# Where the inverse row sums lie for the product that normalises P

## The chip, the core and the metric

The kernel runs on one core of one Trainium2 chip. The metric is device time in microseconds (us), the median of three runs; lower is better. A core has five engines with queues of their own: TensorE (PE in the profile, with its weight loads as PEld), VectorE (DVE), ScalarE (ACT), GpSimd (POOL) and SyncE (SP), which here issues the DMAs. They run side by side and wait for each other through semaphores. Two on-chip memories matter: SBUF, which all of them use, and PSUM, the banks into which matmuls write.

## What is computed

Causal windowed attention with a linear bias per head, and then a soft mixture of experts over all tokens:

```python
scores = scale * q @ k.T                                   # B=8, H=8, S=576, D=64
scores = where((rel >= 0) & (rel < 128), scores + bias, -1e9)
attn = exp(scores - scores.max(-1));  attn /= attn.sum(-1) + 1e-09
x = (attn @ v)            # reshaped to N=4608 tokens x 512
logits = x @ phi          # 32 slots
d = softmax(logits, over tokens);  slot_input = d.T @ x
slot_out[e] = relu(slot_input[e] @ w1[e]) @ w2[e]          # 8 experts x 4 slots
out = softmax(logits, over slots) @ slot_out
```

The change sits in `attn /= attn.sum(...)`.

## The kernel before

A tile is 128 queries of one batch entry (the fifth tile of an entry has 64). A tile's heads are worked in groups of four score matrices, so there are 72 groups; each group is a score tile of 128 x 4 x 128 values that count. The program first runs a loop over the 72 groups, and then a tail with the experts and the output.

The instructions of each engine stand in the order in which the code below calls them; nothing reorders them. In iteration `i` of the loop, with `new` = group i and `old` = group i-1:

- `softmax_front(new, old)`, nearly all on DVE: `merge` (L286) puts the masked halves of the scores together in PSUM, `total` (L309, on POOL) adds 1e-9 to the row sums of `old`, `rowmax` (L300) takes the maximum of each row and writes it, negated, into spare columns of the same PSUM tile, `inverse` (L313) makes reciprocals of the row sums of `old`, `bias` (L304) scales the maxima of `new` into `nb` in SBUF, and `normalise` (L317) multiplies P of `old`, 128 x 512 values in SBUF, by the inverse sums of their rows.
- `flip` and `split` of group i-3: PE transposes P into PSUM (L374), ACT copies it to SBUF (L380), POOL cuts it along the diagonal with two selections (L386, L388).
- `values` of group i-4: the matmuls with V (L410). After the second group of a tile DVE copies the result out (L424).
- `scores` of group i+1: PE (L261, L270).
- `expo(new)`: four exponentials on ACT (L359), each with a sum along its row; each shows as an ACTIVATE and an ACTIVATION_READ_ACCUMULATOR.
- on some iterations, further steps: transposes of finished tiles (L438, copied out at L447), and, when four tiles are finished (a pass), their logits (L456) and a running softmax over tokens (L464 to L522).

The score tile of group i is one of two PSUM tiles, taken in turn; each is two banks:

```python
173 |     s4s = [ps_s.tile([P, 4, 2 * P], F32, name=f"s4_{i}") for i in range(2)]
299 |         st[key]["mx"] = ranges(key, us)[:, :, 4 * P - 2:4 * P]
```

The scores take at most the first 448 of the 512 columns of a bank; the row maxima take the last two. `st[key]["rs"]` is a tile of four columns in SBUF, one of two buffers. Groups 0 and 1 are normalised by other branches (`first`, `eager`), and the last group is normalised behind the loop.

When the program is built, each instruction is given the semaphore waits that its operands need. For a PSUM bank these follow the bank, whatever columns of it are used.

Of the kernel before, what the change touches and what calls it, by code (L numbers as in the profile page):

```python
# [24 lines left out]
P = 128  # L25
# [47 lines left out]
def tile_attn_softmoe(  # L73
# [13 lines left out]
    nc = tc.nc  # L87
# [56 lines left out]
    st = {}  # L144
# [131 lines left out]
    ALL, LO, HI = slice(0, 4), slice(0, 2), slice(2, 4)  # L276
    EVEN, ODD = slice(0, 4, 2), slice(1, 4, 2)

    def merge(key, us=ALL):
        x = ranges(key, us).rearrange("p a (x y) -> p a x y", y=KB)  # L280
        m = x.shape[1]
        if key[1] < 4:
            to, of, keep = x[:, :, 0:6:5], x[:, :, 2:4], bc(mask.bitcast(I32), 1, m)
        else:
            to, of, keep = x[:, :, 0:8:4], x[:, :, 2:8:4], bc(bc(mask[:, 0].bitcast(I32), 1, 2), 1, m)
        nc.vector.copy_predicated(to, keep, of)  # L286
# [9 lines left out]
    def rowmax(key, us):  # L296
        if "nb" not in st[key]:
            st[key]["nb"] = work.tile([P, 4], F32, tag="nb", name="nb")
        st[key]["mx"] = ranges(key, us)[:, :, 4 * P - 2:4 * P]
        nc.vector.tensor_reduce(st[key]["mx"], merged(key, us), axis=AX.X, op=ALU.max, negate=True)  # L300

    def bias(key, us):
        nb = st[key]["nb"][:, us].rearrange("p (a u) -> p a u", u=2)
        nc.vector.tensor_scalar_mul(nb, st[key]["mx"], SCALE)  # L304

    def total(key, us, eng=None):
        if "rs" not in st[key]:
            st[key]["rs"] = work.tile([P, 4], F32, tag="rs", name="rs")
        (eng or nc.vector).tensor_scalar(  # L309
            st[key]["rs"][:, us], st[key]["sm"][:, us], EPS, 1.0, op0=ALU.add, op1=ALU.mult)  # L310

    def inverse(key, us):
        nc.vector.reciprocal(st[key]["rs"][:, us], st[key]["rs"][:, us])  # L313

    def normalise(key, us):
        p4, rs = st[key]["p4"][:, us], st[key]["rs"][:, us]
        nc.vector.tensor_tensor(p4, p4, bc(rs, 2, P), op=ALU.mult)  # L317

    def normalise_first(key, us):
        p4 = st[key]["p4"]  # L320
        for u in range(4)[us]:
            nc.scalar.mul(p4[:, u], p4[:, u], st[key]["rs"][:, u:u + 1])  # L322
# [3 lines left out]
    def filler():  # L326
        if fillers:
            fillers.pop(0)()

    def softmax_front(new, old):  # L330
        first, eager = number[old] == 0, 0 < number[old] < EAGER
        merge(new)
        filler()
        if not eager:
            total(old, ALL, nc.gpsimd)
        if first:
            inverse(old, ALL)
            normalise_first(old, LO)
        rowmax(new, ALL)
        filler()  # L340
        if not first and not eager:
            inverse(old, ALL)
        filler()
        bias(new, ALL)
        if eager:
            total(old, ALL)
            inverse(old, ALL)
        filler()
        normalise(old, HI if first else ALL)
# [262 lines left out]
    sums = area[:, 3]  # L612
# [161 lines left out]
    with tc.manual_schedule(engines=ORDERED):  # L774
        scores(0)
        loads(0)
        for i in range(n):
            new = groups[i]
            run("pre", i)
            if i:  # L780
                softmax_front(new, groups[i - 1])
            else:
                for us in (LO, HI):
                    merge(new, us)
                    rowmax(new, us)
                    bias(new, us)
                    expo(new, us)
            near = int(i < SKIP)
            if i + near >= FLAG and i != SKIP:
                flip(groups[i + near - FLAG])  # L790
                split(groups[i + near - FLAG])
            run("act", i)
            if i + near >= LAG and i != SKIP:
                values(groups[i + near - LAG])
                after_values(i, groups[i + near - LAG])
            if i + 1 < n:
                scores(i + 1)
            if i + 1 < n - 1:
                loads(i + 1)
            if i:  # L800
                expo(new)
            run("pe", i)
            load_weights_at(i)
            run("dve", i)
# [324 lines left out]
```

## Time and profile before

| | |
|---|---|
| median of 3 runs | 286.24 us (286.18 to 286.52) |
| the profiled execution | 286.09 us, of which the span from first to last instruction is 284.3 us |
| granted TensorE clock | 0.992 |
| loop over the groups | up to about 213 us of the span; the tail from there |
| busy share of the span | PE 91%, DVE 77%, ACT 67%, POOL 39% |

The busy shares are means over the loop and the tail. Rows of a timeline read: start in us, duration in us, engine, line, operation, out<-in, and in brackets how long the engine sat idle before and what ended that. An instruction may start some 0.1 us before the one ahead of it on its engine ends, where it need not wait for it.

### The profile page before, as it was taken

How to read it: one execution, taken by the hardware profiler on the slowest of the kernel's cores; microseconds unless marked ns; L12 is line 12 of the kernel's file. 1: busy time of each engine (PE TensorE's matmuls, PEld its weight loads, DVE VectorE, ACT ScalarE, POOL GpSimd, SP SyncE). 2: the span in 40 equal slices, each digit the busy share in tenths (PEclk: the TensorE clock that was granted, in tenths of full speed). 3: DMA queues.
4: the chain of work that ended last, by engine and by line, in shares of the span. 5: the costliest groups of instructions: out<-in, count | busy, mean ns of one | idle time of the engine just before them, and what ended most of it. 6: DMA issues, size and time to landing. Idle time of an engine off the chain costs nothing.

```text
span 284.3 us, 11675 instructions
## 1 busy us (share of the span) xinstructions
PE 257.5 (91%) x4575; PEld 180.7 (64%) x4575; DVE 218.6 (77%) x546; ACT 190.5 (67%) x780; POOL 111.7 (39%) x221
## 2 busy tenths in 40 slices
PE   7789898989899999998989998998989899999990
PEld 3567676767577677676667766766666443587750
DVE  1789998997998898899999899897973352656352
ACT  2868868887798887897897888887774411044460
POOL 3035734481574385265527526556452011000000
PEclk9999999999999999999999999999999999999996
DMA  5735368889786998889698778876565588999997
GB/s 167 238 110 153 115 173 250 255 247 295 252 277 184 303 303 262 257 265 285 221 298 283 255 236 280 268 212 218 166 213 199 172 257 296 417 416 373 376 357 295
DMA packets 36767, 72.49 MB, mean 255 GB/s; under 512 B 4413, under 2 KB 15337, under 8 KB 36713
## 3 DMA queue, kind: packets, MB, share of 16 engines
q1 hardware_dynamic: 35992, 71.25, 75.7%
q8 instruction: 36, 0.59, 0.8%
q10 hardware_dynamic: 720, 0.51, 0.6%
q14 instruction: 19, 0.15, 0.2%
HBM read 62.30 MB, written 9.44 MB: 252 GB/s over the span
## 4 chain that ended last, share of the span: by engine, by line
PE 44%; DVE 38%; ACT 9%; issue 3%; DMA 3%; POOL 1%; DVEq 0%; ACTq 0%; SPq 0%; POOLq 0%
DVE area L317 12%; DVE s L300 9%; PE xp L410 8%; ACT area L359 6%; PE op L967 5%; PE s L270 5%; DVE area L424 5%; PE hp L930 5%; DVE s L286 4%; PE po L992 4%; PE s L261 2%; PE lp L456 2%; PE pq L374 2%; DVE acc L522 2%; DMA area<-v_n 2%
## 5 line engine op out<-in xcount | busy, mean ns | idle before, releaser
L359 ACT ACTIVATE area<-s,nb 128x128 f32<-128x128 f32 x286 | 101.9, 379 | 21.6 <-DVE nb L304 20.2
L410 PE MATMUL xp<-area 128*64 128x128 f32 (+1 forms) x1104 | 71.7, 270 | 9.5 <-DVE area L424 6.6
L410 PEld LDWEIGHTS xp<-area 128*64 128x64 f32 x1104 | 54.5, 137 | 16.4 <-POOL area L388 5.0
L359 ACT ACTIVATION_READ_ACCUMULATOR area<-s,nb 128x1 f32 x286 | 62.2, 218 | 0.0
L317 DVE TENSOR_TENSOR area<-area,rs 128x512 f32<-128x512 f32 (+1 forms) x73 | 59.9, 821 | 1.7 <-ACT area L447 0.4
L270 PE MATMUL s<-kq 64*64 64x192 f32 (+2 forms) x1144 | 57.0, 316 | 0.0
L386 POOL TENSOR_SCALAR_AFFINE_SELECT area<-area 128x512 f32<-128x512 f32 (+1 forms) x57 | 42.7, 748 | 26.9 <-ACT area L380 26.3
L380 ACT COPY area<-pq 128x512 f32<-128x512 f32 (+1 forms) x72 | 42.5, 592 | 16.0 <-PE pq L374 14.3
L300 DVE TENSOR_REDUCE s<-s 128x4 f32<-128x512 f32 (+1 forms) x72 | 50.0, 694 | 2.2
L388 POOL TENSOR_SCALAR_AFFINE_SELECT area<-area 128x512 f32<-128x512 f32 (+1 forms) x57 | 46.5, 817 | 3.9
L270 PEld LDWEIGHTS s<-kq 64*64 64x64 f32 x1144 | 41.2, 139 | 3.4
L309 POOL TENSOR_SCALAR rs<-sm 128x4 f32<-128x4 f32 x70 | 13.5, 193 | 71.2 <-ACT area L359 69.8
L286 DVE COPY_PREDICATED s<-cst,s 128x256 f32<-128x256 int32 (+1 forms) x72 | 30.2, 419 | 4.8 <-PE s L270 4.4
L374 PE MATMUL pq<-unit_r,area 64*128 64x64 f32 x552 | 31.4, 234 | 1.9 <-ACT area L322 1.2
L374 PEld LDWEIGHTS pq<-unit_r,area 64*128 64x128 f32 x552 | 23.0, 140 | 11.6 <-issue 5.0
L261 PE MATMUL s<-ramp,pair_of 64*64 64x384 bf16 x286 | 27.0, 358 | 2.5 <-ACT area L359 2.0
L424 DVE COPY area<-xp 128x512 f32<-128x512 f32 (+1 forms) x38 | 24.1, 633 | 3.6 <-PE xp L410 3.4
L447 ACT COPY area<-pq 128x512 f32<-128x512 f32 x34 | 20.2, 594 | 0.3 <-PE pq L432 0.3
L261 PEld LDWEIGHTS <-pair_of 64*64 64x64 bf16 x288 | 9.5, 106 | 15.7 <-issue 12.0
L438 PEld LDWEIGHTS pq<-unit_r,area 64*128 64x128 f32 x264 | 10.7, 138 | 13.2 <-issue 11.7
L994 ACT COPY ob<-po 128x512 f32<-128x512 f32 x19 | 10.4, 592 | 11.4 <-PE po L992 11.4
L994 DVE COPY ob<-po 128x512 f32<-128x512 f32 x17 | 11.2, 686 | 6.6 <-PE po L992 4.4
(164 smaller groups left out, 276.6 us busy)
## 6 DMA issues: line engine op xcount, KB each, us to landing
w<-w SPq DMA_DIRECT2D x53, 512.0 KB, 5.4
out<-ob SPq DMA_DIRECT2D x36, 256.0 KB, 3.6
kq<-q_t SPq DMA_DIRECT2D x69, 128.0 KB, 3.3
kq<-k_t SPq DMA_DIRECT2D x32, 256.0 KB, 3.4
area<-v_n SPq DMA_DIRECT2D x31, 256.0 KB, 4.5
area<-w SPq DMA_DIRECT2D x8, 512.0 KB, 4.9
area<-v_n SPq DMA_DIRECT2D x12, 128.0 KB, 5.2
kq<-w SPq DMA_DIRECT2D x3, 512.0 KB, 5.6
```

The source lines that it names most:

```text
L261: nc.tensor.matmul(dst[strip], lhsT=pair_of[rows, int(t == 0), strip], rhs=src, start=True, stop=False)
L270: nc.tensor.matmul(parts[par][KB * jj:KB * jj + KB, second * u + KB * skip:second * u + WIN], lhsT=qt[rows, jj if t < 4 else j, KB * h:KB ...
L286: nc.vector.copy_predicated(to, keep, of)
L300: nc.vector.tensor_reduce(st[key]["mx"], merged(key, us), axis=AX.X, op=ALU.max, negate=True)
L317: nc.vector.tensor_tensor(p4, p4, bc(rs, 2, P), op=ALU.mult)
L359: nc.scalar.activation(s["p4"][:, u], src, AF.Exp, bias=s["nb"][:, u:u + 1], scale=SCALE, accum_out=s["sm"][:, u:u + 1],)
L374: nc.tensor.transpose(s["pt"][:, 2 * (u % 2) + u // 2, r], s["p4"][rows, u], ident[rows, rows])
L380: nc.scalar.copy(pa[:, us].rearrange("p u (r w) -> p u r w", r=2), s["pt"][:, us])
L386: nc.gpsimd.affine_select(prev, own, [[-step, m], [0, 4], [-1, KB]], ALU.is_gt, 0.0, base=-i0, channel_multiplier=1)
L388: nc.gpsimd.affine_select(own, own, [[step, m], [0, 4], [1, KB]], ALU.is_ge, 0.0, base=i0, channel_multiplier=-1)
L410: nc.tensor.matmul(xp[D * par:D * par + D, j, 0:w], lhsT=v_slot[b, t - 1 + ph][:, D * h:D * h + D], rhs=src[:, :, par, i] if t < 4 else sr ...
L424: nc.vector.tensor_copy(dst, src[:, :, 0:w])
```

## The change

For the groups that the loop normalises in the common branch, the reciprocal no longer overwrites the row sums in SBUF: it reads them there and writes the inverse sums into columns 504 to 507 of the first bank of the score tile of `new`, the group in front. `normalise` then reads P of `old` from SBUF and the inverse sums from PSUM. Group 0, group 1 and the last group keep the sums in SBUF, so 69 of the 72 groups are changed.

```diff
-    def inverse(key, us):
-        nc.vector.reciprocal(st[key]["rs"][:, us], st[key]["rs"][:, us])
+    def inverse(key, us, beside=None):
+        sums = st[key]["rs"]
+        if beside is not None:
+            st[key]["rs"] = st[beside]["s4"][:, 0, 4 * P - 8:4 * P - 4]
+        nc.vector.reciprocal(st[key]["rs"][:, us], sums[:, us])
...
         if not first and not eager:
-            inverse(old, ALL)
+            inverse(old, ALL, new)
```

No instruction is added, removed or moved. The waits differ. Of DVE, one group in the middle of the loop, before (`s_1_84` is one of the two score tiles; the name of a semaphore is that of the engine waited for; the row of `L317` is the product):

```order
L286 COPY_PREDICATED s_1_84<-cst,s_1_84 128x2x2x64 [waits PE_49]
L300 TENSOR_REDUCE s_1_84<-s_1_84 128x2x2 [waits DVE_49]
L313 RECIPROCAL rs<-rs 128x4 [waits Pool_49]
L304 TENSOR_SCALAR nb<-s_1_84 128x4 [waits DVE_49]
L317 TENSOR_TENSOR area<-area,rs 128x512 [waits DVE_49,Activation_49]
```

Here the reciprocal waits for POOL alone, the bias for the row maximum, and the product for the reciprocal and for P. The same place in the changed program, where the code lies three lines lower:

```order
L286 COPY_PREDICATED s_1_84<-cst,s_1_84 128x2x2x64 [waits PE_49]
L300 TENSOR_REDUCE s_1_84<-s_1_84 128x2x2 [waits DVE_49]
L316 RECIPROCAL s_1_84<-rs 128x4 [waits DVE_49,Pool_49]
L304 TENSOR_SCALAR nb<-s_1_84 128x4 [waits DVE_49]
L320 TENSOR_TENSOR area<-area,s_1_84 128x512 [waits Activation_49]
```

The reciprocal now also waits for the row maximum, which writes the same bank; the bias waits for the reciprocal; the product, behind the bias, needs no wait on DVE any more. On ACT the rows read the same in both programs, `ACTIVATE area,sm<-s` with a wait for DVE, but the count that the first exponential of a group waits for differs: before, it is that of the bias of its group (L304), in the changed program that of the product (L320), which is one higher, in all 69 changed groups. The exponentials read the same bank in which the inverse sums lie. The matmuls of the scores of a later group, which overwrite the tile, wait for the exponentials as before.

## Prediction

> **What bounds the kernel now.** I read the page first, then the waits, the groups of instructions by shape, and the timeline of a few groups. The page says that the loop is shared by three engines, with DVE nearly as long on the chain that ended last as PE:
>
> ```profile
> PE 257.5 (91%) x4575; PEld 180.7 (64%) x4575; DVE 218.6 (77%) x546; ACT 190.5 (67%) x780; POOL 111.7 (39%) x221
> PE 44%; DVE 38%; ACT 9%; issue 3%; DMA 3%; POOL 1%; DVEq 0%; ACTq 0%; SPq 0%; POOLq 0%
> DVE area L317 12%; DVE s L300 9%; PE xp L410 8%; ACT area L359 6%; PE op L967 5%; PE s L270 5%; DVE area L424 5%; PE hp L930 5%; DVE s L286 4%; PE po L992 4%; PE s L261 2%; PE lp L456 2%; PE pq L374 2%; DVE acc L522 2%; DMA area<-v_n 2%
> ```
>
> The change lies in the loop, whose pace I take from the first exponential of each group. That of group 2 starts at 12.40 and that of group 71 at 210.03, so 69 periods take 197.63 us, 2.864 us each:
>
> ```profile
> 12.40 0.40 ACT L359 ACTIVATE area<-s,nb 128x128 f32<-128x128 f32 x1
> 210.03 0.37 ACT L359 ACTIVATE area<-s,nb 128x128 f32<-128x128 f32 x1 [0.61 <-DVE nb L304]
> 12.40:210.03 197.63, 185.66 (x3606) 135.40 (x3600) 179.53 (x438) 160.63 (x700) 103.40 (x193) 1.00 0.74 233
> ```
>
> The last row is that stretch as a window: length, then busy time of PE, PEld, DVE, ACT and POOL, granted clock and DMA share. PE is busy 185.7 us of 197.6, or 2.69 per group: a pace of 2.7 to 2.9 is PE's, and the periods swing around it. What ACT waits for:
>
> ```profile
> ACT area L359 <- DVE nb L304: 20.2, 31, 1.1
> POOL rs L309 <- ACT area L359: 69.8, 54, 6.1
> DVE rs L313 <- POOL rs L309: 2.8, 10, 0.9
> ```
>
> The exponentials wait for the bias in 31 groups, 20.2 us in all. POOL's sum waits for the exponentials, and the reciprocal rarely waits for POOL. So a ring exponentials, sum, reciprocal is there, but it isn't closed: the next exponentials wait for the bias alone, which needs neither.
>
> **The change part by part.** *The wait that closes the ring.* The first exponential of a group now waits for the product of its iteration. The product needs the inverse sums of the group before, so its exponentials must have ended. I price one round from two neighbouring groups, first DVE, then ACT, POOL, and DVE of the second:
>
> ```profile
> 123.83 0.42 DVE L286 COPY_PREDICATED s<-cst,s 128x256 f32<-128x256 int32 x1
> 124.29 0.70 DVE L300 TENSOR_REDUCE s<-s 128x4 f32<-128x512 f32 x1
> 124.89 0.17 DVE L313 RECIPROCAL rs<-rs 128x4 f32<-128x4 f32 x1
> 125.02 0.16 DVE L304 TENSOR_SCALAR nb<-s 128x4 f32<-128x4 f32 x1
> 125.17 0.76 DVE L317 TENSOR_TENSOR area<-area,rs 128x512 f32<-128x512 f32 x1
> ...
> 125.28 0.37 ACT L359 ACTIVATE area<-s,nb 128x128 f32<-128x128 f32 x1
> ...
> 126.57 0.21 ACT L359 ACTIVATION_READ_ACCUMULATOR area<-s,nb 128x1 f32 x1
> 126.66 0.60 ACT L380 COPY area<-pq 128x512 f32<-128x512 f32 x1
> 127.12 0.62 ACT L447 COPY area<-pq 128x512 f32<-128x512 f32 x1
> ...
> 126.87 0.19 POOL L309 TENSOR_SCALAR rs<-sm 128x4 f32<-128x4 f32 x1 [0.42 <-ACT area L359]
> ...
> 127.09 0.18 DVE L313 RECIPROCAL rs<-rs 128x4 f32<-128x4 f32 x1
> ```
>
> From the first exponential (125.28) to the end of the reciprocal that its sums feed (127.09 + 0.18 = 127.27) is 1.99 us: exponentials to 126.78, POOL's sum to 127.06, reciprocal. The bias now waits for that reciprocal; a DVE instruction that waits for the one ahead starts 0.04 after its end (merge to 124.25, row maximum at 124.29), and the bias takes 0.16. The product starts 0.01 before the bias ends (125.18, 125.17). It takes 0.69, below. ACT follows DVE by 0.10 (bias ends at 125.18, exponential at 125.28). Sum: 1.99 + 0.04 + 0.16 - 0.01 + 0.69 + 0.10 = 2.97 us, the least that a period can be. It is above the mean period of 2.864, so no gain elsewhere can win it back: 69 x 2.97 = 204.9, against 197.6: **+7.3 us**.
>
> *The product itself.* Its prices by shape, and those of the nearest operations with one operand in PSUM:
>
> ```profile
> L317 DVE TENSOR_TENSOR area<-area,rs 128x512 f32<-128x512 f32 x70 | 58.7, 838 | 1.4 <-ACT area L447 0.4
> L522 DVE SCALAR_TENSOR_TENSOR acc<-acc,al,ap 128x512 f32<-128x512 f32 x6 | 4.4, 738 | 0.0
> L537 DVE TENSOR_TENSOR ln<-dp,cm 128x128 f32<-128x128 f32 x7 | 2.0, 292 | 0.2
> L317 DVE TENSOR_TENSOR area<-area,rs 128x256 f32<-128x256 f32 x3 | 1.3, 422 | 0.2
> ```
>
> The mean of 838 ns mixes quiet and disturbed ones, as three places show:
>
> ```profile
> 121.96 0.69 DVE L317 TENSOR_TENSOR area<-area,rs 128x512 f32<-128x512 f32 x1
> 122.16 1.01 POOL L386 TENSOR_SCALAR_AFFINE_SELECT area<-area 128x512 f32<-128x512 f32 x1 [0.51 <-ACT area L380]
> 123.24 0.66 POOL L388 TENSOR_SCALAR_AFFINE_SELECT area<-area 128x512 f32<-128x512 f32 x1
> ...
> 127.57 0.66 POOL L386 TENSOR_SCALAR_AFFINE_SELECT area<-area 128x512 f32<-128x512 f32 x1
> 127.73 1.03 DVE L317 TENSOR_TENSOR area<-area,rs 128x512 f32<-128x512 f32 x1 [0.41 <-ACT area L447]
> ```
>
> Whichever of product and selection starts first keeps its short time (0.69, 0.66), and the other is stretched to about 1.0. Undisturbed, L317 takes 0.69 for 512 elements and 0.42 for 256 (the x3 row): 0.27 for 256, or 1.05 ns an element. L537 is the same operation with one operand in PSUM and takes 292 ns for 128; at 512 it would take 292 + 384 x 1.05 = 695 ns. So I take 0.69. Below it a product can't come, since no row of this shape does; above it lie the 0.74 of L522, which does two operations on an operand in PSUM (+0.05 x 69 = +3.5 us), and 0.84 if the disturbance stays (+0.15 x 69 = +10.4). On this the Trainium skill, "SBUF — State Buffer", section "Who interferes with whom", says that a DVE instruction with two SBUF inputs contends with a GpSimd instruction that reads SBUF, and that one with at most one SBUF input doesn't. The rows above agree with the first half; no row here shows the second. By it the product is 0.69 always and POOL's selections are 0.66; without it the sum would be up to the +10.4 dearer.
>
> *The wait of the reciprocal for the row maximum.* Before, it started 0.10 before the row maximum ended; now 0.04 after. Where the row maximum is the later one, the bias is delayed from 125.02 to about 125.24; this lies beside the ring, in which the reciprocal's release by POOL comes later. It costs nothing as long as merge and row maximum are done 1.8 us after the last exponentials began, and DVE has that time: after a product it has merge and row maximum, 1.16, and in every second group the copy of L424, 0.68, which makes 1.84 with some overlap:
>
> ```profile
> L424 DVE COPY area<-xp 128x512 f32<-128x512 f32 x31 | 21.1, 682 | 3.6 <-PE xp L410 3.4
> ```
>
> With its cover gone (a pass adds steps on DVE too) it would cost what exceeds 1.8, a few tenths in a few groups.
>
> *The write to PSUM* of 4 columns instead of SBUF: the bias, which reads PSUM, takes 0.16, the reciprocal 0.17; I take no difference, bounds -0.02 to +0.03 a round, 2 us either way.
>
> *What ACT and POOL do in the ring's wait.* Between its exponentials ACT has 2.97 - 1.50 = 1.47 us for the copies L380 and L447, 0.60 and 0.62 with overlap; they fit. POOL's two selections start behind L380 and take 1.32; they are done before the next sum.
>
> *Uneven iterations.* The ring is a floor for each period, while PE's work is not even. Where a pass closes, two iterations of PE read
>
> ```profile
> 85.19:88.94 3.75, 3.75 (x86) 2.91 (x85) 2.90 (x6) 2.34 (x10) 1.72 (x4) 1.00 0.60 200
> 88.94:91.61 2.67, 2.67 (x64) 2.08 (x62) 2.44 (x7) 2.67 (x14) 1.34 (x3) 1.00 0.55 145
> ```
>
> 6.42 us of PE against 2 x 2.97 = 5.94: 0.48 too much. Before, periods shorter than the floor made up for such places; now there are none. Eight passes close in the loop: 8 x 0.48 = **+3.8 us**. From below it is 0: PE's mean of 2.69 leaves 0.28 free in each round, and two more rounds take the excess in if PE can work that far ahead. From above, if no iteration lends another anything, each of the 69 periods is the larger of its old length and 2.97. Summed over the 70 starts, of which the first and the last stand above, that adds 18.2 us, ring included.
>
> *The tail* runs unchanged code. *Sum*: the profiled execution's 286.09 + 7.3 + 3.8 = 297.2 us. That execution lies 0.15 below the median of the runs, which I leave out.
>
> Of the wait itself the Trainium skill says, in "PSUM — Partial Sum Buffer", section "PSUM bank collisions raise a hardware error", that two engines must not touch the same bank and quadrant in the same cycle, reads against reads included. By it the new wait can't be spared and the sum is 297.2; without it exponentials and product could overlap as now, and nothing would be lost. No row of this trace shows two engines in one bank at once.
>
> **The rivals.** (1) *Ring alone*: PE gets far enough ahead that passes cost nothing, 293.4 us. For it: PE has 2.69 of work per 2.97. Against: the 3.75. (2) *No lending at all*: 286.1 + 18.2 = 304.3 us. For it: 24 of the 69 old periods, by the same starts, are longer than 2.97. Against: many of these were long because PE was behind, which slower neighbours mend. (3) *The product stays disturbed* or costs more from PSUM: 0.84 instead of 0.69 makes 307.6. Against: L537. In the new order product and selections begin within 0.1 us of each other, so it would matter. (4) *Faster*: the undisturbed product shortens DVE. L317 has 12% of the chain, 34 us, and loses (838 - 690)/838 of it: 6.0 us, for 280.1. This decides only if the ring takes less than the old period, so if it is 0.11 shorter than my 2.97, for instance because POOL's sum and the reciprocal came early. The rows 126.78 to 127.27 speak against it. (5) *Nothing measurable*: the exponentials were behind the product's end already in 11 of those 70 groups, and would have to be in all.
>
> **How the numbers follow.** Forecast around 297 (294.5 to 301): 0.46. Ring alone (291 to 294.5): 0.22. No lending (301 to 305.5): 0.15. Product dearer (305 to 309): 0.08. Faster: 0.05. Nothing: 0.04. A change of less than 0.2%, 0.57 us, can't be told from none. Slower sums to 0.91. For 8 in 10 the range takes the forecast, the ring alone and most of no lending: 291.0 to 304.0.
>
> **What would show it.** Right: in the trace after, exponentials released by the product L320, with ACT idle before them for much of 204.9 + 3.8 - 160.6 (ACT's work in the window above) = 48 us, instead of 20.2 by the bias; periods with a hard floor near 2.97; the product at 0.69 with little spread; the selections near 0.66; the busy time of PE unchanged and its share lower. Wrong: periods of 2.3 to 2.8 as before, a product whose mean stays at 838, or a loop that ends at its old time.

## The result and the profile after

The changed kernel takes 299.34 us (median of 6 runs, 297.51 to 301.68) against 286.21 us before, a ratio of 1.046 (95% interval 1.042 to 1.050): 13 us slower. The profiled execution took 298.5 us, its span is 296.8 us, 12.5 us more than before. Of the runs below, one of e1_other_bank (306.68 us) and one of e7_later_extras (292.45 us) lie far above the others of their kernel and are left out of the medians and ratios. The page's shares of the changed kernel, and its chain by engine and by line:

```profile
PE 259.0 (87%) x4575; PEld 183.1 (62%) x4575; DVE 211.9 (71%) x546; ACT 191.4 (64%) x780; POOL 97.4 (33%) x221
...
PE 37%; DVE 28%; ACT 19%; POOL 6%; issue 5%; DMA 3%; DVEq 0%; SPq 0%; ACTq 0%; POOLq 0%
ACT area L362 17%; DVE area L320 8%; PE xp L413 7%; PE op L970 5%; PE hp L933 5%; DVE s L300 5%; PE s L270 4%; PE po L995 3%; DVE area L427 3%; DVE s L316 3%; DVE nb L304 2%; POOL rs L309 2%; DVE s L286 2%; POOL area L389 2%; PE s L261 2%
```

DVE has 6.7 us less to do than before and POOL 14.3 us less, and still the program is longer: the exponentials, which had 6% of the chain, have 17%, and POOL's small sum is on it. The first exponentials of groups 2 and 71, and the window between them:

```profile
12.03 0.40 ACT L362 ACTIVATE area<-s,nb 128x128 f32<-128x128 f32 x1
222.28 0.37 ACT L362 ACTIVATE area<-s,nb 128x128 f32<-128x128 f32 x1 [1.42 <-DVE area L320]
12.03:222.28 210.25, 189.79 (x3618) 140.30 (x3614) 173.40 (x438) 161.46 (x701) 90.11 (x194) 0.98 0.71 221
```

A round, or period, is the time from the first exponential of one group to that of the next, and is named here by the group at its end. The 69 rounds take 210.25 us, 12.6 more than the 197.63 before, so the loss lies in the loop and the tail lost nothing. What waits there:

```profile
POOL rs L309 <- ACT area L362: 101.0, 65, 5.7
ACT area L362 <- DVE area L320: 41.5, 56, 1.4
DVE s L316 <- POOL rs L309: 23.9, 45, 0.9
```

The 20.2 us for the bias have become 41.5 us for the product, and the reciprocal now waits for POOL in 45 rounds. One round, ACT, then POOL, then DVE:

```profile
88.06 0.37 ACT L362 ACTIVATE area<-s,nb 128x128 f32<-128x128 f32 x1 [0.42 <-POOL area L389]
...
89.36 0.21 ACT L362 ACTIVATION_READ_ACCUMULATOR area<-s,nb 128x1 f32 x1
...
90.96 0.37 ACT L362 ACTIVATE area<-s,nb 128x128 f32<-128x128 f32 x1 [0.91 <-DVE area L320]
...
89.66 0.19 POOL L309 TENSOR_SCALAR rs<-sm 128x4 f32<-128x4 f32 x1 [0.88 <-ACT area L362]
90.12 0.66 POOL L389 TENSOR_SCALAR_AFFINE_SELECT area<-area 128x512 f32<-128x512 f32 x1 [0.27 <-ACT area L383]
...
89.89 0.19 DVE L316 RECIPROCAL s<-rs 128x4 f32<-128x4 f32 x1 [0.25 <-POOL rs L309]
90.11 0.16 DVE L304 TENSOR_SCALAR nb<-s 128x4 f32<-128x4 f32 x1
90.19 0.68 DVE L320 TENSOR_TENSOR area<-area,s 128x512 f32<-128x512 f32 x1
```

Each starts when the one before has ended: exponentials to 89.57, sum to 89.85, reciprocal to 90.08, product to 90.87, next exponentials at 90.96. That is a closed ring of 2.90 us. Of the 69 periods 48 lie between 2.85 and 2.98, 2.90 in the mean, and none is shorter, where the kernel before had 45 below 2.97. The other 21 are longer, by 10.3 us in all over 2.895. DVE in one of the long ones, 3.41 us, from one reciprocal to the product of the next round:

```profile
102.14 0.19 DVE L316 RECIPROCAL s<-rs 128x4 f32<-128x4 f32 x1 [0.84 <-POOL rs L309]
102.36 0.16 DVE L304 TENSOR_SCALAR nb<-s 128x4 f32<-128x4 f32 x1
102.44 0.68 DVE L320 TENSOR_TENSOR area<-area,s 128x512 f32<-128x512 f32 x1
103.04 0.68 DVE L427 COPY area<-xp 128x512 f32<-128x512 f32 x1
103.64 0.74 DVE L525 SCALAR_TENSOR_TENSOR acc<-acc,al,ap 128x512 f32<-128x512 f32 x1
104.29 0.42 DVE L286 COPY_PREDICATED s<-cst,s 128x256 f32<-128x256 int32 x1
104.75 0.70 DVE L300 TENSOR_REDUCE s<-s 128x4 f32<-128x512 f32 x1
105.56 0.19 DVE L316 RECIPROCAL s<-rs 128x4 f32<-128x4 f32 x1
105.78 0.16 DVE L304 TENSOR_SCALAR nb<-s 128x4 f32<-128x4 f32 x1
105.85 0.68 DVE L320 TENSOR_TENSOR area<-area,s 128x512 f32<-128x512 f32 x1
```

DVE first stands idle for 0.84, since it must have POOL's sum, and then, behind the reciprocal, has six instructions in a row, with gaps of 0.04 at most, and the next reciprocal 0.11 behind them. It can't do the copy and `slot_add` (L525) in the idle time, since they stand behind the product in its queue.

In all 21 long rounds the reciprocal starts 0.10 after the row maximum has ended, so it is DVE that comes last there, and not POOL's sum. In 18 of them the merge follows an instruction of DVE with at most 0.03 of idle time, and one of a pass's steps stands ahead of it: these rounds are DVE's queue and are 7.3 us longer than the floor in all (in three of them a step of the pass had itself waited 0.08 to 0.18 for PE). In the other three, those of groups 3, 4 and 68, DVE sits idle before the merge until PE's scores are there; they make 3.0 us. The merges of these three, and the wait of PE ahead of the last:

```profile
13.61 0.43 DVE L286 COPY_PREDICATED s<-cst,s 128x256 f32<-128x256 int32 x1 [0.79 <-PE s L270]
17.03 0.43 DVE L286 COPY_PREDICATED s<-cst,s 128x256 f32<-128x256 int32 x1 [1.18 <-PE s L270]
210.31 0.43 DVE L286 COPY_PREDICATED s<-cst,s 128x256 f32<-128x256 int32 x1 [1.62 <-PE s L270]
208.64 0.66 PE L413 MATMUL xp<-area 128*64 128x128 f32 x8 [1.03 <-DMA area<-v_n]
```

The operand itself did what it could. First all changed products, by minimum, median and maximum; then POOL's selections, in the changed kernel and in the one before:

```profile
L320 DVE TENSOR_TENSOR area<-area,s x69: 677/677/679, 15.2 to 221.5; 128x512 f32<-128x512 f32 x69
```

```profile
L389 POOL TENSOR_SCALAR_AFFINE_SELECT area<-area 128x512 f32<-128x512 f32 (+1 forms) x57 | 37.3, 654 | 19.1 <-ACT area L383 18.8
L391 POOL TENSOR_SCALAR_AFFINE_SELECT area<-area 128x512 f32<-128x512 f32 (+1 forms) x57 | 37.5, 657 | 3.9
```

```profile
L386 POOL TENSOR_SCALAR_AFFINE_SELECT area<-area 128x512 f32<-128x512 f32 (+1 forms) x57 | 42.7, 748 | 26.9 <-ACT area L380 26.3
L388 POOL TENSOR_SCALAR_AFFINE_SELECT area<-area 128x512 f32<-128x512 f32 (+1 forms) x57 | 46.5, 817 | 3.9
```

At 90.19 above, product and selection run side by side for 0.59 us, and both keep their short times. With two operands in SBUF one of the two was stretched in the rows of before, the selection to 1.01 or the product to 1.03.

### The profile page after: what moved, and what is told of

Read it like the earlier page. It is cut to its first block, busy times and chain, and to the rows that moved or that the text cites. A ratio compares the mean times of both kernels' runs of the same rounds, so it can differ in the third digit from the quotient of the medians.

```text
span 296.8 us, 11658 instructions
## 1 busy us (share of the span) xinstructions
PE 259.0 (87%) x4575; PEld 183.1 (62%) x4575; DVE 211.9 (71%) x546; ACT 191.4 (64%) x780; POOL 97.4 (33%) x221
## 4 chain that ended last, share of the span: by engine, by line
PE 37%; DVE 28%; ACT 19%; POOL 6%; issue 5%; DMA 3%; DVEq 0%; SPq 0%; ACTq 0%; POOLq 0%
ACT area L362 17%; DVE area L320 8%; PE xp L413 7%; PE op L970 5%; PE hp L933 5%; DVE s L300 5%; PE s L270 4%; PE po L995 3%; DVE area L427 3%; DVE s L316 3%; DVE nb L304 2%; POOL rs L309 2%; DVE s L286 2%; POOL area L389 2%; PE s L261 2%
## 5 line engine op out<-in xcount | busy, mean ns | idle before, releaser
L362 ACT ACTIVATE area<-s,nb 128x128 f32<-128x128 f32 x286 | 101.4, 367 | 45.5 <-DVE area L320 41.5
L413 PEld LDWEIGHTS xp<-area 128*64 128x64 f32 x1104 | 55.7, 139 | 15.7 <-POOL area L391 6.8
L362 ACT ACTIVATION_READ_ACCUMULATOR area<-s,nb 128x1 f32 x286 | 58.2, 204 | 0.0
L270 PE MATMUL s<-kq 64*64 64x192 f32 (+2 forms) x1144 | 56.3, 313 | 0.2 <-DMA kq<-k_t 0.2
L320 DVE TENSOR_TENSOR area<-area,s 128x512 f32<-128x512 f32 x69 | 46.7, 677 | 0.0
L389 POOL TENSOR_SCALAR_AFFINE_SELECT area<-area 128x512 f32<-128x512 f32 (+1 forms) x57 | 37.3, 654 | 19.1 <-ACT area L383 18.8
L391 POOL TENSOR_SCALAR_AFFINE_SELECT area<-area 128x512 f32<-128x512 f32 (+1 forms) x57 | 37.5, 657 | 3.9
L261 PE MATMUL s<-ramp,pair_of 64*64 64x384 bf16 x286 | 26.3, 351 | 10.0 <-ACT area L362 8.9
L316 DVE RECIPROCAL s<-rs 128x4 f32<-128x4 f32 x69 | 12.8, 186 | 26.3 <-POOL rs L309 23.9
L261 PEld LDWEIGHTS <-pair_of 64*64 64x64 bf16 x288 | 10.7, 104 | 22.7 <-issue 18.5
L427 DVE COPY area<-xp 128x512 f32<-128x512 f32 (+1 forms) x38 | 24.1, 635 | 0.0
```

The lines of the kernel that those rows point to most:

```text
L261: nc.tensor.matmul(dst[strip], lhsT=pair_of[rows, int(t == 0), strip], rhs=src, start=True, stop=False)
L270: nc.tensor.matmul(parts[par][KB * jj:KB * jj + KB, second * u + KB * skip:second * u + WIN], lhsT=qt[rows, jj if t < 4 else j, KB * h:KB ...
L362: nc.scalar.activation(s["p4"][:, u], src, AF.Exp, bias=s["nb"][:, u:u + 1], scale=SCALE, accum_out=s["sm"][:, u:u + 1],)
L389: nc.gpsimd.affine_select(prev, own, [[-step, m], [0, 4], [-1, KB]], ALU.is_gt, 0.0, base=-i0, channel_multiplier=1)
L391: nc.gpsimd.affine_select(own, own, [[step, m], [0, 4], [1, KB]], ALU.is_ge, 0.0, base=i0, channel_multiplier=-1)
L413: nc.tensor.matmul(xp[D * par:D * par + D, j, 0:w], lhsT=v_slot[b, t - 1 + ph][:, D * h:D * h + D], rhs=src[:, :, par, i] if t < 4 else sr ...
```

## The experiments

The theory was: the wait of the exponentials for the product closes a ring, and the ring is the cost. The rivals were the operand in PSUM as such, two engines in one bank, any delay of the exponentials whether or not it closes a ring, and PE's uneven work.

**The sums in the other bank** (e1_other_bank).

```diff
-            st[key]["rs"] = st[beside]["s4"][:, 0, 4 * P - 8:4 * P - 4]
+            st[key]["rs"] = st[beside]["s4"][:, 1, 4 * P - 8:4 * P - 4]
```

> The changed kernel with the inverse sums in the second bank of the score tile instead of the first (columns 504 to 507 there). The first two exponentials read the first bank alone. The built program makes the first exponential wait for the product all the same. Theory wait: same time as the changed kernel, 297 to 301, floor 2.9. Rival bank (two engines in one bank at once is what costs, on the chip itself): faster, since the first two exponentials no longer share a bank with the product, 288 to 294.

Measured: 299.05 us, ratio to the kernel before 1.043 (1.035 to 1.051), as the changed kernel. The exponentials wait for the product 41.5 us in 56 rounds, the same to the tenth. The first exponential of a group reads the first bank and the product the second, and still, in 67 of the 69 changed rounds, the exponential starts 0.09 after the product has ended, as in the changed kernel. So in the built program the wait follows the whole score tile of two banks. The remark ahead of the prediction, that waits follow the bank, was too narrow. The place inside the tile doesn't matter; whether two engines can read one bank at once is not tested by any run here, since the wait keeps them apart.

**The bias ahead of the reciprocal** (e2_bias_first).

```diff
+        bias(new, ALL)
         if not first and not eager:
             inverse(old, ALL, new)
         filler()
-        bias(new, ALL)
```

> The changed kernel with the bias (L304) ahead of the reciprocal; the exponentials still wait for the product. Theory ring (each round runs exponentials, sum on POOL, reciprocal, product, exponentials; floor 2.89 us in the trace): the round loses the bias between reciprocal and product, 0.12 - 0.04 = 0.08 us, in about 52 rounds, and gains some 0.06 in the 17 rounds that wait for DVE instead: -3 us, about 296. Rival operand (what costs is the product or the reciprocal touching PSUM, not the order): no change, 299. Rival DVE load (DVE's sum of work sets the pace): no change, 299.

Measured: 303.84 us, ratio 1.063 (1.056 to 1.069), 4.5 us slower than the changed kernel. A miss in sign. The timeline of DVE shows why:

```profile
112.19 0.70 DVE L300 TENSOR_REDUCE s<-s 128x4 f32<-128x512 f32 x1
112.93 0.16 DVE L304 TENSOR_SCALAR nb<-s 128x4 f32<-128x4 f32 x1
113.19 0.18 DVE L316 RECIPROCAL s<-rs 128x4 f32<-128x4 f32 x1
113.48 0.69 DVE L320 TENSOR_TENSOR area<-area,s 128x512 f32<-128x512 f32 x1
```

The product starts 0.11 after the reciprocal it waits for has ended (113.37, 113.48), and so it did with the bias in between (90.08, 90.19): the bias lay in that gap at no cost, and nothing was to be won in the ring's rounds. The shortest is 2.88 here and 2.89 in the changed kernel. In rounds led by the row maximum, three instructions now wait for each other instead of two, and from its end to the product it takes 0.59 (112.89, 113.48) instead of 0.40 (105.45, 105.85). The long rounds became 26 and their excess 13.2 us. So there are two kinds of rounds, and what is put between row maximum and product lengthens the second. Of the 5.2 us between the two profiled executions the loop has 3.5; the tail, whose code is unchanged, has 1.6.

**The wait alone** (e3_wait_alone), the kernel before with sums in SBUF.

```diff
-        bias(new, ALL)
+        if first or eager:
+            bias(new, ALL)
...
         normalise(old, HI if first else ALL)
+        if not first and not eager:
+            bias(new, ALL)
```

> The kernel before, sums in SBUF, but the bias stands behind the product on DVE, so that the exponentials wait for the product through the bias; no operand moves. Theory ring: slower by as much as the change or more, since the product is the disturbed one of 0.69 to 1.19 us and the bias adds 0.15: floor 3.0 to 3.3, 298 to 305 us. Rival operand (the PSUM operand costs): 286, as before.

Measured: 317.85 us, ratio 1.113 (1.104 to 1.122). The ring costs without any operand in PSUM, and more than the 298 to 305 expected, because here product and selection meet in most rounds:

```profile
L317 DVE TENSOR_TENSOR area<-area,rs x73: 416/1146/1185, 10.1 to 243.5; 128x512 f32<-128x512 f32 x70, 128x256 f32<-128x256 f32 x3
```

The median product is 1146 ns against 695 in the kernel before; 40 of the 73 take more than 1.0 us, against 16 before. Both hang on the exponentials' end, one through the sum, the other through the copy of P. With the bias behind the product the shortest round is 2.95, and with 0.47 us more in the product most rounds take 3.41; only 17 stay below 2.98. So in the changed kernel the operand saved much of what the wait would otherwise have cost.

**Two steps of a pass behind the row maximum** (e4_extras_behind_max): the changed kernel with

```diff
         rowmax(new, ALL)
+        run("mid", number[new])
...
-            do("pre", i + 4, slots_max, k)
+            do("mid", i + 4, slots_max, k)
...
-            do("dve", i + 5, slot_add, k)
+            do("mid", i + 6, slot_add, k)
```

> The changed kernel with two DVE steps of a pass, slot_add (0.74 us) and slots_max (0.57), moved from ahead of the merge to behind the row maximum, where DVE waits for POOL's sum in most rounds. Theory DVE queue (the 17 rounds longer than the floor, 10.5 us in all, are those in which DVE's steps behind the product hold up merge and row maximum): two rounds per pass lose about 0.4 us each, 6 us less, 292 to 296. Theory PE (uneven work of PE sets these rounds, as the prediction had it): no change, 299.

Measured: 295.98 us, ratio 1.036 (1.030 to 1.041), 3.4 us less than the changed kernel, at the upper end of what was expected; the same instructions, on the same engine, in its idle time. 47 rounds stay at 2.90, and the excess of the others falls from 10.3 to 7.3 us. So the long rounds are at least in part DVE's queue, as PE's work is unchanged. Of what remains, rounds 3, 4 and 68, in which DVE waits for PE, still have 2.8 us; round 65 has joined them, with 0.5. In most of the other long rounds a moved step, now between row maximum and reciprocal, ends after POOL's sum and holds the reciprocal up.

**The ring opened** (e5_one_round_later): the changed kernel, but the group two back is normalised, so that its sums are a round old.

```diff
+        i = number[new]
+        done = old if i < SKIP else groups[i - 2] if i > SKIP else None
...
-        if not first and not eager:
-            inverse(old, ALL, new)
+        if not first and not eager and done:
+            inverse(done, ALL, new)
...
-        normalise(old, HI if first else ALL)
+        if done:
+            normalise(done, HI if first else ALL)
```

Behind the loop, `inverse` and `normalise` of the last but one group follow.

> The changed kernel, but from iteration 8 on each iteration normalises the group two back instead of one back, beside the scores of the new group; the last but one group is normalised behind the loop. Each product still stands ahead of the exponentials, which still wait for it, but its sums were ready a round earlier: the ring is open. Theory ring: the floor of 2.89 goes, back to 284 to 291 us. Rival any wait (it is enough that the exponentials start 0.68 later than the bias): stays at 296 to 300.

Measured: 287.94 us, ratio 1.005 (1.002 to 1.008), 11 us less than the changed kernel. The product is as short as there, and the exponentials still wait for it:

```profile
ACT area L365 <- DVE area L320: 27.0, 36, 1.5
```

But 37 periods are below 2.85 now. With the same wait but the ring open, the floor is gone, and the time is back near that of the kernel before. How much of that the ring alone accounts for needs the control that follows.

**The control in SBUF** (e6_later_in_sbuf): the same edit on the kernel before.

> The kernel before, sums in SBUF, with the normalising of the group two back instead of one back: the control of e5. The exponentials wait for the bias alone, and the product reads two SBUF operands. Theory ring: the kernel before had no closed ring, so nothing is won by the delay: 284 to 288, at most 1 us more for the product that now stands behind the loop. If the operand in PSUM saves DVE and POOL time that counts, this is slower than e5; if the wait in e5 costs more than that, faster.

Measured: 280.20 us, ratio 0.979 (0.973 to 0.986), the fastest of all, 6 us below the kernel before, which was not expected. Its chain by engine, its products, and what the exponentials wait for:

```profile
PE 72%; DVE 11%; ACT 6%; DMA 4%; issue 3%; POOL 2%; DVEq 0%; ACTq 0%; POOLq 0%
```

```profile
L317 DVE TENSOR_TENSOR area<-area,rs x73: 415/690/1185, 9.9 to 207.4; 128x512 f32<-128x512 f32 x70, 128x256 f32<-128x256 f32 x3
```

```profile
ACT area L362 <- DVE nb L304: 14.0, 26, 0.9
```

The chain is PE's, 72% instead of 44%, and DVE's share falls from 38% to 11%. Two things differ on DVE from the kernel before: the reciprocal waits for POOL 0.9 us in all instead of 2.8, as its sums are a round old, and the products are less often disturbed, with a mean of 759 ns instead of 821 over all 73. The exponentials wait 14.0 us for the bias instead of 20.2. Which of the two matters more was not tried.

The control limits what e5 says. Taking the sums a round later wins 6 us in SBUF too, where no ring was closed. Where the group one back is normalised the move to PSUM costs 13.1 us, and where the group two back is, 7.7. If the effects of the two edits add up, closing the ring accounts for 5.4 of the 13.1. The rest is what the move costs where no ring is closed, so the rival of any wait, exponentials that start only behind the product, isn't out for this part; no run separates it from the operand's other waits. That the ring paces the changed kernel itself is shown by its 48 rounds at 2.90 with none shorter, and not by this difference.

Against this kernel e5 pays 7.7 us, of which 6.7 lie in the loop of the profiled executions: it differs by the operand and the waits that come with it, so the shorter product is worth less than what those waits cost, even with the ring open. Products here still reach 1185 ns; what that costs was not tried.

**Both edits together** (e7_later_extras is e5 with the edit of e4, e8_sbuf_later_extras is e6 with it).

> e5 (sums in PSUM, two groups back) with slot_add and slots_max behind the row maximum as in e4. With an open ring DVE doesn't idle there, so less is won than e4's 3.4 us: 284 to 288. Theory DVE queue: some gain from token steps that no longer hold up the merge; theory PE: no change against e5, 288.

Measured: 288.45 us, ratio 1.007 (1.003 to 1.011).

> e6 (sums in SBUF, two groups back) with slot_add and slots_max behind the row maximum. Here these steps delay the bias and with it the exponentials, as DVE isn't waiting: 284 to 289, no more than 1 us off e6.

Measured: 281.82 us, ratio 0.984 (0.979 to 0.988). Neither is better than without the edit, and both miss what was expected: e7 lies just above 284 to 288, and e8 is 1.6 us slower than e6, where at most 1 was foreseen. So the 3.4 us that e4 won depend on the idle time that the ring leaves on DVE; with the ring open, moving the two steps wins nothing.

## Why the prediction was right or wrong

The forecast was 297.2 us with 291.0 to 304.0; 299.34 was measured, and the mechanism was the one forecast: the wait of L362 for L320, the ring through POOL's sum, a hard floor, the waits for the product at 41.5 us where 48 us of idle time were foreseen. But two terms of the sum were off, in opposite directions.

- *The ring, +7.3.* The floor is 2.895, not 2.97, so the ring alone is 69 x 2.895 - 197.63 = 2.1 us. The working put the bias into the ring with 0.19 between reciprocal and product, having seen the product start right as the bias ended at 125.18. In the trace after, 0.11 lies between them: the bias starts 0.03 after the reciprocal, and the product 0.08 before the bias ends, where the working took 0.04 and 0.01. In e2, with no bias between them, it is 0.11 too, so the bias adds nothing there. The rest, 2.02 to the end of the reciprocal, 0.68 for the product and 0.09 to the exponentials, came within 0.03 of what was read.
- *Uneven iterations, +3.8.* They cost 10.3 us. The step that failed is the one that took PE's work at the end of a pass for what makes rounds uneven. The longer of the two iterations of PE from which it was priced lies in the round of group 29, which was 3.96 before and is 2.89 after:

```profile
85.26 0.37 ACT L359 ACTIVATE area<-s,nb 128x128 f32<-128x128 f32 x1 [0.65 <-DVE nb L304]
89.22 0.39 ACT L359 ACTIVATE area<-s,nb 128x128 f32<-128x128 f32 x1
```

```profile
90.96 0.37 ACT L362 ACTIVATE area<-s,nb 128x128 f32<-128x128 f32 x1 [0.91 <-DVE area L320]
93.85 0.37 ACT L362 ACTIVATE area<-s,nb 128x128 f32<-128x128 f32 x1
```

So PE's excess there was taken in, as the bound from below had it. PE does make three rounds long, by 3.0 us, but two of them at the start of the loop and one behind a wait for a DMA. The sentence on the reciprocal's wait for the row maximum named the right place, DVE's merge and row maximum with L427 and a pass's steps ahead of them, but gave it "a few tenths in a few groups"; it is 0.2 to 0.7 in 18 rounds, 7.3 us in all. e4 won 3.4 us by moving DVE steps alone.

- *The product at 0.69*: right, 0.677, less than the 695 ns worked out from L537. The rival *product stays disturbed* is out. By the Trainium skill, "SBUF — State Buffer", section "Who interferes with whom", a DVE instruction with at most one SBUF input doesn't contend with GpSimd, outside modes that `tensor_tensor` doesn't have. The trace agrees: 69 products between 677 and 679 ns, 56 of them beside selections of 0.66.
- *ACT and POOL in the ring's wait*: right. The profile puts 3.9 us of idle time before exponentials down to POOL, in 7 rounds, 88.06 above among them, but there too they start 0.09 after the product has ended.
- *The rival "faster"* fell: the 6.7 us that DVE saved don't count where the ring or the queue sets the time. It needed a ring 0.11 shorter than 2.97; this one was 0.075 shorter. *Ring alone*, 293.4, and *no lending*, 304.3, were both computed with the floor of 2.97; with 2.895 they are 288.2 and, by the same starts, 301.0.
- *The tail*: unchanged, as said.

So the total was near because an overestimate of 5.2 us and an underestimate of 6.5 us nearly cancel. The wait and the ring were foreseen; that the sum came so near was luck.

## What to carry to other kernels

Before moving an operand into a buffer that other engines read, list who will now wait for whom, and see whether the new wait closes a ring through the next iteration; a ring is a floor for each round, and here the time saved on the engines inside the loop didn't buy it back. The wait has a price of its own, too: with the ring open the move to PSUM still cost 7.7 us. Price the ring by the releases as well as the durations, since small instructions can hide in the gap of a wait. And where a value is needed one round after it is made, taking it two rounds later can be worth more than making its use cheaper: here that, with the sums left in SBUF, is the version that beats both kernels.

## What the runs showed of the hardware

A product of 128 x 512 with its second operand in PSUM takes 677 ns, with hardly any spread, 13 ns less than the undisturbed one with both in SBUF (690); it was expected to cost a few ns more. A DVE instruction that waits for the one right ahead started 0.04 us after it in the case of merge and row maximum (104.71, 104.75), but 0.11 after for reciprocal and product (113.37, 113.48 in e2). The tail, from the first exponential of group 71, takes 76.1 to 76.3 us in the profiled executions of e1, e2 and e5, with a granted clock of 0.94 to 0.95 in it, and 74.2 to 74.9 at 0.96 to 0.98 in the other seven. In the first 37.1 us of the profiled run the granted TensorE clock was 0.86, and in the loop 0.98, where before it was 1.00:

```profile
0.00:37.10 37.10, 28.68 (x438) 19.71 (x438) 24.58 (x67) 22.63 (x96) 11.80 (x34) 0.86 0.50 150
```

From the third round on, the rounds in this stretch are at 2.9 us like the later ones. The first two, 3.86 and 3.49, wait for PE's scores, whose matmuls took 1.54 and 1.49 us instead of the 0.82 of the third. In the kernel before they took 1.54 and 1.36 as well, with a granted clock of 1.00 from 12 to 20 us, so what the lower clock cost can't be read off; why it was lower is open.
